# The product of q with k'v as four 64 by 64 tiles side by side, with w_in's rows permuted to match

## The chip, the cores and the metric

The kernel runs on one core of one Trainium2 chip. The metric is the device time of an execution in microseconds. The engines are named as in the profile: PE (TensorE's matmuls), PEld (its weight loads), DVE (VectorE), ACT (ScalarE), POOL (GpSimd) and SP (SyncE, which issues most of the transfers).

## The reference

Linear attention feeds a gated feed-forward layer. In float32 for the attention; the two weight matrices are float64:

```python
# q, k, v: (8 batches, 8 heads, 576 tokens, 64)
q_s = exp(q - q.max(-1));  q_s = q_s / (q_s.sum(-1) + 1e-09)     # softmax over d
k_s = exp(k - k.max(2));   k_s = k_s / (k_s.sum(2) + 1e-09)      # softmax over tokens
kv = np.einsum('bhsd,bhse->bhde', k_s, v)                        # 64 x 64 per head
x = np.einsum('bhsd,bhde->bhse', q_s, kv)
x = x.transpose(0, 2, 1, 3).reshape(4608, 512)                   # column = head * 64 + e
h = x @ w_in                                                     # w_in: 512 x 2048
g = h * erf(softplus(h))
out = g @ w_out                                                  # w_out: 2048 x 512
```

## The kernel before

**Two computations run interleaved.** The feed-forward layer goes over 48 items. An item n is a pair of batches, a block of 384 tokens (three blocks make the pair's 1152) and a quarter of the 2048 hidden columns. It has mm1 (x times its part of w_in, into the banks pX, pY, pZ), the gate in three steps (T: softplus, G: erf, both on ACT; U: the multiplication by h on DVE) and mm2 (into the banks o). The first six items use float32 matmuls (`mm1_32` at L996, mm2 at L1074); the rest split each operand into two fp16 halves and use three passes (L957, L1083). Attention for the batches b = 0 to 7 runs between: `kv_mm` (L548, 64-column tiles), `kv_norm` (L567 to L577), `kv_max`, `kv_split` (L590), the transposes of q, `x_mm` (L654) and `x_split`, in which ACT takes x out of PSUM (L449) and the fp16 halves are made.

**q times k'v.** Two heads share a block of 128 rows: x's column block c holds heads 2c and 2c + 1. `kvbd` is block diagonal: a 128 by 128 tile per c with one head's 64 by 64 k'v in the upper left, the other's in the lower right, and zeros, which POOL fills (L113, and once more at L596). `x_mm` makes one column block: q transposed (128 rows of d for two heads, 512 tokens) against that tile. For b = 0 and 1 it is one float32 matmul (L657), which the trace shows as two records; from b = 2 it is three fp16 matmuls (L660). 64 more tokens of each of two batches, the tails, are done once per pair in `tails()`, into one bank `xt`. The banks for the transposes, for x and for xt come from a pool of two (`bank`).

**The weights** come as 16 pieces of 1 MB: of w_in 256 rows by 512 columns, of w_out 256 rows. `wload` loads them, the first eight on SP's queue, the rest on POOL's, and `wdecode` on DVE turns each piece's pairs of 32-bit words into float32 (three operations, L215, L218, L221, each for 1 MB). Piece j.a is half a of the j-th job; the jobs alternate: in 0, in 1, out 0, in 2, out 1, in 3, out 2, out 3. In the prediction D2.0 or "piece 2.0" is the first half of job 2, w_out's first.

**What sets the order.** Up to item 5 the program is written out by hand in the string ORDER: a token is one step (D: decode, m: a quarter of mm1, M: a third of mm2, x: `x_mm` of batch 0, y: the rest of its split, Q: sums of squares of weights, A: the next piece of attention). After it a loop runs item by item, and `pace` takes as many pieces of attention as the numbers in SHARES say. The tile scheduler then sets the order of each engine's queue, so one step written elsewhere can move others. Every engine goes through its queue in order.

Of the kernel before, what the change touches and what calls it, by code (L numbers as in the profile page):

```python
# [8 lines left out]
F16 = mybir.dt.float16  # L9
F32 = mybir.dt.float32  # L10
# [21 lines left out]

ORDER = """
    kmax qm0 kT kB qe0 qm1 ks2 ks0 ks1 ke2 ke0 ke1 qn0 t0 t1 qe1 qn1 w6 kv0 kn0 kv1 kn1
    D0.0.0 D0.1.0 t2 t3 x0 x1 x2 x3 kvs lkv y0 y1 y2 y3
    m0.0 m0.1 D0.0.1 D0.1.1 D1.0 D1.1 m0.2 m0.3 T0 G0 Q0
    D2.0 A m1.0 D2.1 m1.1 U0 m1.2 m1.3 T1 G1 Q1 A A D3.0 M0.0 D3.1 M0.1 M0.2 Q2 U1 A A
    m2.0 D4.0 m2.1 D4.1 m2.2 m2.3 T2 G2 Q3 A A D5.0 M1.0 D5.1 M1.1 M1.2 U2 A A Q4 D6.0
# [18 lines left out]
def attn_moe_kernel(  # L57
# [9 lines left out]
    nc = tc.nc  # L67
# [95 lines left out]
    def wload():  # L163


        i = nxt[0]
        while i < NPC * NJ and slots:
            w = slots.pop(0)
            if i >= NPC * (NJ - 1 if w is None else NJ if w < 2 else w - 2):
                continue  # L170
            if w == -1:
                w, other = None, "x7"
            else:
                other = None
            which, g = wjobs[i // NPC]
            a = i % NPC
            if which == "in":
                src = w_in[a * 2 * P:(a + 1) * 2 * P, 2 * g * 512:2 * (g + 1) * 512]
            else:
                src = w_out[(4 * g + 2 * a) * P:(4 * g + 2 * a + 2) * P, :]  # L180
            if other:

                raws[i] = xp.tile([P, 2, 1024], I32, tag=other, name=f"raw_{i}")
            elif w is None:
                raws[i] = rw.bitcast(I32).rearrange("p (a n) -> p a n", a=2)
            else:
# [258 lines left out]
    def bank(name):  # L445
        return psa.tile([P, 512], F32, tag="bk", name=name)

    def x_put(src, x, s):
        nc.scalar.activation(x, src, AF.Copy, scale=2.0**-QS if s is None else s)  # L449
# [35 lines left out]
    def load_q(b, hf):  # L485
        bat[b].setdefault("q", {})[hf] = load_half(q, "q", b, hf)
# [67 lines left out]


    E32, QDMA = 2, 3
    kv32 = [t.rearrange("p h c e -> p (h c e)").bitcast(F32) for t in kvbd]
    kv32 = [t.rearrange("p (c e) -> p c e", c=NC4) for t in kv32]

    def kv_norm(b, hf, bk):  # L560
        if b >= E32:
            if hf == 0:
                bat[b]["kvf"] = asc[:, 0, :NC4 * D].rearrange("p (c e) -> p c e", c=NC4)
            kvf = bat[b]["kvf"]
# [5 lines left out]
        if b >= E32:  # L570
            nc.vector.tensor_tensor(
                kvf[:, cs, :], bkv[:, :, :D], rd.to_broadcast([P, 2, D]), op=ALU.mult
            )
            return
        for a in range(2):
            ps = slice(a * D, (a + 1) * D)
            nc.vector.tensor_tensor(  # L577
                kv32[b][ps, cs, ps], bkv[ps, :, :D], rd[ps].to_broadcast([D, 2, D]),
                op=ALU.mult,
            )  # L580

    def kv_max(b):
        mx = at.tile([P, 1], F32, tag="mx", bufs=1, name=f"mx_{b}")
        nc.vector.tensor_reduce(
            mx, (kv32[b] if b < E32 else bat[b]["kvf"]).rearrange("p c e -> p (c e)"), axis=AX.X,
            op=ALU.max, apply_absolute_value=True,
        )
        return mx

    def kv_split(b, mx):  # L590

        d = bat[b]
        s, u = scale_of_max(mx, f"x{b}")
        d["sx"], d["ux"] = s, u
        if 2 <= b < 4:
            nc.gpsimd.memset(kvbd[b % 2], 0.0)  # L596
        for a in range(2 if b >= E32 else 0):
            kvf = d["kvf"]
            ps = slice(a * D, (a + 1) * D)
            hi, lo = (kvbd[b % 2][ps, i, :, ps] for i in range(2))  # L600
            nc.vector.tensor_scalar_mul(hi, kvf[ps], s[ps])
            nc.vector.scalar_tensor_tensor(
                lo, kvf[ps], s[ps], hi, op0=ALU.mult, op1=ALU.subtract
            )
# [45 lines left out]
    def q_T(b, c, bk):  # L650
        q_cols(b, c, bk)
        return q_evac(b, c % 2, bk)

    def x_mm(b, c, out_, qT):  # L654

        if b < E32:
            nc.tensor.matmul(out_, kv32[b][:, c, :], qT[:, 0], start=True, stop=True)  # L657
            return
        for i, (wl, ql) in enumerate(((0, 0), (0, 1), (1, 0))):
            nc.tensor.matmul(  # L660
                out_, kvbd[b % 2][:, wl, c, :], qT[:, ql], start=(i == 0), stop=(i == 2)
            )

    def x_split(b, c, bk, part=None):
        for blk, off, o, w in xcols(b, 0 if b % 2 == 0 else SM + 2 * TAIL, SM)[part or slice(9)]:
            x_put(
                bk[:, o:o + w], xblock(blk)[:, c, off:off + w],
                1.0 if blk == 0 else bat[b]["sx"] if b < E32 else None,
            )

    def attention(b):
# [50 lines left out]
        def tails():  # L722
            if b < QDMA:
                bk = bank(f"qTt_{p}")
                for c in range(NC4):
                    nc.tensor.transpose(
                        bk[:, c * P:(c + 1) * P], hd(even["qt"])[:, c * P:(c + 1) * P], ident
                    )
                even["qtT"] = q_evac(b, 0, bk)
            yield SHARES[9]  # L730
            qT = even["qtT"]
            bk = bank(f"xt_{p}")
            x = xblock(p * NBK + 1)
            bk3 = bk.rearrange("p (c s) -> p c s", c=NC4)
            for a in range(2):
                for c in range(NC4):
                    cs = slice(c * P + a * TAIL, c * P + (a + 1) * TAIL)
                    x_mm(2 * p + a, c, bk[:, cs], qT[:, :, cs])
            for a in range(2 if b < E32 else 1):
                w = TAIL if b < E32 else P  # L740
                o = SM - T + a * TAIL
                x_put(
                    bk3[:, :, a * TAIL:a * TAIL + w], x[:, :, o:o + w],
                    bat[a]["sx"] if b < E32 else None,
                )
# [36 lines left out]
    def start():  # L782
# [51 lines left out]
        def xc(c):
            name = f"x_0_{c}"
            bk = pso.tile([P, 512], F32, tag=f"o{c}", name=name) if c < 3 else bank(name)
            x_mm(0, c, bk, r[f"t{c}"])
            x_split(0, c, bk, slice(1))
            put(f"x{c}", bk)

        def put(key, val):
            r[key] = val
# [392 lines left out]
```

## Time and profile before

| | |
|---|---|
| median of three runs | 847.01 us (846.93 to 848.13) |
| the profiled execution's own time | 847.39 us |
| its span in the profile | 845.4 us |
| granted clock of TensorE | 1.0 |
| DMA, whole span | 61.53 MB, mean 73 GB/s |
| w_in's first pieces on SP's queue, issue to landing | 10.6 us (median of 4) |

The span runs from the first to the last instruction of the profiled execution; its time holds about 2 us around that. Rows of groups read: line, engine, operation, result and operands, shapes, count; busy time in us and mean ns of one; idle time of the engine before them and what ended it. Timeline rows read: start in us, us, engine, line, operation. Neighbouring matmuls overlap, so one's own cost is the distance of the starts.

### The profile page before, as it was taken

To read this page: it belongs to the slowest core of one execution; us is meant where nothing else is said; L and a number is where in the kernel's file an instruction comes from. 1 tells how busy PE (TensorE), PEld (TensorE's weight loads), DVE (VectorE), ACT (ScalarE), POOL (GpSimd) and SP (SyncE) were. 2 spreads that over 40 slices of the span, in tenths; PEclk is the share of its full clock that TensorE was granted. 3 is DMA by queue.
4 is the path that set the end of the run, shared out by engine and by line. 5 is a ranking of instruction groups with operands and counts; after the bars stand their busy time and mean duration, and the time that the engine had idled before them with its cause. 6 is when DMAs were issued, how large, how long until landed. Compare 5 with 4: busy or idle time off the path is not lost.

```text
span 845.4 us, 15123 instructions
## 1 busy us (share of the span) xinstructions
PE 817.5 (97%) x6336; PEld 554.3 (66%) x6336; DVE 631.9 (75%) x900; ACT 506.6 (60%) x638; POOL 18.1 (2%) x37
## 2 busy tenths in 40 slices
PE   3999999999999999999999999999999999999996
PEld 2655555666766766766776776766776776767662
DVE  6899689998998869867877769867876657553543
ACT  2597659876674567465665467465665475544532
POOL 2101100000000000000000000000000000000000
PEclk9999999999999999999999999999999999999999
DMA  9975920023226303411171203411131100100100
GB/s 267 403 189 168 210 52 38 1 58 75 63 51 127 88 19 76 106 38 27 46 151 30 76 19 76 106 39 26 40 74 13 40 1 1 39 1 2 38 1 38
DMA packets 141347, 61.53 MB, mean 73 GB/s; under 512 B 130528, under 2 KB 132576, under 8 KB 141280
## 3 DMA queue, kind: packets, MB, share of 16 engines
q1 hardware_dynamic: 139104, 52.18, 24.9%
q0 software_dynamic: 2176, 8.39, 2.9%
q8 instruction: 50, 0.82, 0.4%
q14 instruction: 17, 0.14, 0.1%
HBM read 45.09 MB, written 9.44 MB: 64 GB/s over the span
## 4 chain that ended last, share of the span: by engine, by line
PE 66%; DVE 16%; ACT 10%; DMA 3%; issue 3%; SPq 1%; POOL 0%; ACTq 0%; DVEq 0%; POOLq 0%
PE o L1083 28%; PE pX L957 15%; PE pZ L957 8%; PE o L1074 4%; ACT G L350 3%; PE pY L957 3%; ACT L350 3%; DVE G L1037 2%; PE kv L548 2%; DVE H L1055 2%; DMA q<-in_q_dram 1%; PE x L660 1%; SPq L415 1%; ACT wt L301 1%; DVE wt L302 1%
## 5 line engine op out<-in xcount | busy, mean ns | idle before, releaser
L1083 PE MATMUL o<-wt,H 128*128 128x512 f16 x1512 | 347.4, 379 | 1.8 <-DVE H L1051 1.3
L957 PEld LDWEIGHTS <-wt 128*128 128x128 f16 x3528 | 294.0, 98 | 29.3 <-issue 5.6
L1083 PEld LDWEIGHTS <-H 128*128 128x128 f16 x1512 | 145.9, 98 | 150.8 <-DVE H L1051 1.8
L957 PE MATMUL pX<-x,wt 128*128 128x192 f16 x2016 | 193.9, 246 | 1.8 <-ACT H L976 0.7
L350 ACT ACT_TABLE_LOAD x105 | 134.7, 1283 | 3.2 <-DVE H L982 1.2
L1037 DVE SCALAR_TENSOR_TENSOR G<-G,small,H 128x1536 f32<-128x1536 f32 x44 | 79.9, 1817 | 46.2 <-ACT G L350 45.9
L984 ACT COPY H<-pX 128x384 f32<-128x384 f32 x42 | 20.0, 477 | 136.8 <-PE pX L957 131.4
L957 PE MATMUL pZ<-x,wt 128*128 128x192 f16 x1008 | 98.2, 246 | 0.0
L350 ACT ACTIVATE G<-H,U 128x768 f32<-128x768 f32 (+1 forms) x56 | 69.3, 1255 | 22.1 <-DVE H L982 21.5
L1055 DVE TENSOR_TENSOR H<-G,H 128x1536 f16<-128x1536 f32 x42 | 73.8, 1756 | 1.0
L350 ACT ACTIVATE G<-G 128x1536 f32<-128x1536 f32 x48 | 71.3, 1486 | 0.5
L449 ACT ACTIVATE x<-x 128x384 f32<-128x384 f32 (+1 forms) x52 | 17.7, 388 | 59.4 <-PE x L660 56.9
L957 PE MATMUL pY<-x,wt 128*128 128x192 f16 x504 | 48.4, 246 | 0.0
L982 DVE TENSOR_TENSOR H<-pZ,H 128x384 f32<-128x384 f32 x42 | 23.2, 553 | 28.9 <-PE pZ L957 28.9
L301 ACT ACTIVATE x<-x 128x768 f16<-128x768 f32 (+1 forms) x44 | 32.9, 762 | 16.4 <-DVE x L394 16.3
L969 DVE COPY H<-pY 128x384 f32<-128x384 f32 x42 | 23.3, 554 | 25.8 <-PE pY L957 25.8
L1051 DVE CAST H<-G 128x1536 f16<-128x1536 f32 x42 | 40.2, 957 | 0.8
L302 DVE SCALAR_TENSOR_TENSOR x<-x,x 128x768 f16<-128x768 f32 (+1 forms) x44 | 37.4, 853 | 3.2 <-ACT x L301 3.2
L1099 DVE TENSOR_SCALAR ob<-o,V 128x512 f32<-128x512 f32 x29 | 21.7, 749 | 21.9 <-PE o L1083 21.8
L996 PE MATMUL pX<-x,wt 128*128 128x384 f32 x96 | 33.9, 488 | 0.0
L971 DVE TENSOR_TENSOR H<-pX,H 128x384 f32<-128x384 f32 x42 | 23.3, 555 | 13.3 <-PE pX L957 12.5
L460 DVE TENSOR_REDUCE q_m<-q 128x16 f32<-128x1024 f32 x14 | 17.1, 1219 | 17.9 <-DMA q<-in_q_dram 17.9
(182 smaller groups left out, 851.1 us busy)
## 6 DMA issues: line engine op xcount, KB each, us to landing
out_dram<-ob SPq DMA_DIRECT2D x32, 256.0 KB, 2.3
vbuf<-in_v_dram SPq DMA_DIRECT2D x60, 128.0 KB, 3.2
q<-in_q_dram SPq DMA_DIRECT2D x56, 128.0 KB, 3.3
k<-in_k_dram SPq DMA_DIRECT2D x56, 128.0 KB, 3.4
wt<-in_moe_w_out_dram POOLq DMA_DIRECT2D x5, 1024.0 KB, 8.7
wt<-in_moe_w_in_dram SPq DMA_DIRECT2D x4, 1024.0 KB, 10.6
wt<-in_moe_w_out_dram SPq DMA_DIRECT2D x2, 1024.0 KB, 15.6
H_raw<-in_k_dram SPq DMA_DIRECT2D x2, 512.0 KB, 5.0
```

The source lines that it names most:

```text
L301: nc.scalar.activation(hi, src, AF.Copy, scale=s)
L302: nc.vector.scalar_tensor_tensor(lo, src, s, hi, op0=ALU.mult, op1=ALU.subtract)
L350: i = nc.scalar.activation(out_, in_, func, **kw)
L957: nc.tensor.matmul(o, w[wl][:, c, a * P:(a + 1) * P], x[:, xl, xi, c, :], start=(new and a == 0 and c == 0 and i == 0), stop=(c == 1 and i ...
L969: nc.vector.tensor_copy(C[0, 0], bank2("Y"))
L971: add(C[0, 0], bank2("X"), C[0, 0], op=ALU.add)
L996: nc.tensor.matmul(ph[:, :T], w[:, c, a * P:(a + 1) * P], x[:, c, :], start=(c == 0), stop=(c == NC4 - 1),)
L1037: nc.vector.scalar_tensor_tensor(flat(s["G"]), flat(s["G"]), GA32 if n < N32 else GA[:, g:g + 1], flat(s["H"]), op0=ALU.mult, op1=ALU.mult,)
L1051: nc.vector.tensor_copy(flat(s["gh"]), flat(s["G"]))
L1055: nc.vector.tensor_tensor(flat(s["gl"]), flat(s["G"]), flat(s["gh"]), op=ALU.subtract)
L1074: nc.tensor.matmul(o, s["G"][:, a, ts_], w[:, a, :], start=(first_ and a == 0), stop=(last_ and a == FG - 1),)
L1083: nc.tensor.matmul(o, s[gt][:, a, ts_], w[wl][:, a, :], start=(first_ and a == 0 and i == 0), stop=(last_ and a == FG - 1 and i == 2),)
```

## The change

`kvbd` becomes `kvh`, which is dense: the 128 partitions hold two heads' 64 rows each, with 64 columns and no zeros. `x_mm` now makes two column blocks, a half hf of x, at once: each pass has four matmuls of 64 rows by 64 columns, one per head. Head 2c + a takes row half a of PE, column half c, and writes bank a. So bank a's partitions hold head a of the first block and head a of the second: the order of x's columns within a half is changed, and w_in's rows are loaded in that order, each piece by two transfers of 64 partitions where one of 128 did it. `kv_norm` is one operation on 128 partitions, `kv_split` two. `x_split` of both blocks follows the product. The loop over the column blocks becomes one over the halves: two transposed q's, then the product. The tails use two banks. In ORDER the tokens x1 and x3 go, and x0 and x2 wait for two transposes each.

```diff
-    D0.0.0 D0.1.0 t2 t3 x0 x1 x2 x3 kvs lkv y0 y1 y2 y3
+    D0.0.0 D0.1.0 t2 t3 x0 x2 kvs lkv y0 y1 y2 y3
...
-    kvbd = []
-    for i in range(2):
-        t = cp.tile([P, 2, NC4, P], F16, name=f"kvbd{i}")
-        nc.gpsimd.memset(t, 0.0)
-        kvbd.append(t)
+    kvh = [cp.tile([P, 2, NC4, D], F16, name=f"kvh{i}") for i in range(2)]
...
-            eng.dma_start(raws[i], src.rearrange("(a p) n -> p a n", p=P))
+            if which == "in":
+                for c in range(2):
+                    eng.dma_start(
+                        raws[i][c * D:(c + 1) * D],
+                        src[c * P:(c + 1) * P].rearrange("(a p) n -> p a n", p=D),
+                    )
+            else:
+                eng.dma_start(raws[i], src.rearrange("(a p) n -> p a n", p=P))
...
-        for a in range(2):
-            ps = slice(a * D, (a + 1) * D)
-            nc.vector.tensor_tensor(
-                kv32[b][ps, cs, ps], bkv[ps, :, :D], rd[ps].to_broadcast([D, 2, D]),
-                op=ALU.mult,
-            )
+        nc.vector.tensor_tensor(
+            kvf[:, cs, :], bkv[:, :, :D], rd.to_broadcast([P, 2, D]), op=ALU.mult
+        )
...
-        if 2 <= b < 4:
-            nc.gpsimd.memset(kvbd[b % 2], 0.0)
-        for a in range(2 if b >= E32 else 0):
-            kvf = d["kvf"]
-            ps = slice(a * D, (a + 1) * D)
-            hi, lo = (kvbd[b % 2][ps, i, :, ps] for i in range(2))
-            nc.vector.tensor_scalar_mul(hi, kvf[ps], s[ps])
+        if b >= E32:
+            hi, lo = (kvh[b % 2][:, i] for i in range(2))
+            nc.vector.tensor_scalar_mul(hi, d["kvf"], s)
...
-    def x_mm(b, c, out_, qT):
-
-        if b < E32:
-            nc.tensor.matmul(out_, kv32[b][:, c, :], qT[:, 0], start=True, stop=True)
-            return
-        for i, (wl, ql) in enumerate(((0, 0), (0, 1), (1, 0))):
-            nc.tensor.matmul(
-                out_, kvbd[b % 2][:, wl, c, :], qT[:, ql], start=(i == 0), stop=(i == 2)
-            )
+    def x_mm(b, hf, outs, qTs):
+
+        passes = ((0, 0),) if b < E32 else ((0, 0), (0, 1), (1, 0))
+        for i, (wl, ql) in enumerate(passes):
+            for c in range(2):
+                for a in range(2):
+                    ps = slice(a * D, (a + 1) * D)
+                    w = kv32[b][ps, 2 * hf + c] if b < E32 else kvh[b % 2][ps, wl, 2 * hf + c]
+                    nc.tensor.matmul(
+                        outs[a][c * D:(c + 1) * D], w, qTs[c][ps, ql],
+                        start=(i == 0), stop=(i == len(passes) - 1),
+                    )
...
-        for c in range(NC4):
-            hf, c2 = divmod(c, 2)
-            if c == 2 and j == 1 and b >= QDMA:
+        for hf in range(2):
+            if hf == 1 and j == 1 and b >= QDMA:
                 yield from tails()
...
-            bk = bank(f"x_{b}_{c}")
-            x_mm(b, c, bk, qT)
...
+            bks = [bank(f"x_{b}_{hf}_{a}") for a in range(2)]
+            x_mm(b, hf, bks, qTs)
...
-            x_split(b, c, bk)
-            if c == NC4 - 1:
+            for a in range(2):
+                x_split(b, 2 * hf + a, bks[a])
+            if hf == 1:
                 d["xdone"] = True
-            yield SHARES[12]
+            yield 2 * SHARES[12]
```

The scheduler's order moves with it, in places that the diff doesn't touch. The first is DVE's queue while item 0 is at its gate; wt are buffers of weights, G and H item 0's gate and mm1. Before, the multiplication of G by H stands behind pieces 2.0, 2.1 and most of what follows:

```order
L215 TENSOR_SCALAR wt_95<-wt_96 128x1024
L218 SCALAR_TENSOR_TENSOR wt_95<-wt_96,wt_95 128x1024
L215 TENSOR_SCALAR wt_95<-wt_97 128x1024
L221 SCALAR_TENSOR_TENSOR wt_95<-wt_96,wt_95 128x1024
L218 SCALAR_TENSOR_TENSOR wt_95<-wt_97,wt_95 128x1024
L215 TENSOR_SCALAR wt_96<-wt_98 128x1024
L221 SCALAR_TENSOR_TENSOR wt_95<-wt_97,wt_95 128x1024
L218 SCALAR_TENSOR_TENSOR wt_96<-wt_98,wt_96 128x1024
L215 TENSOR_SCALAR wt_97<-rw 128x1024
L1034 TENSOR_TENSOR G_377<-G_377,H_337 128x1536
```

In the changed kernel the same place on DVE, from piece 2.0 on (here wt_93):

```order
L220 TENSOR_SCALAR wt_93<-wt_94 128x1024
L1044 TENSOR_TENSOR G_384<-G_384,H_343 128x1536
L223 SCALAR_TENSOR_TENSOR wt_93<-wt_94,wt_93 128x1024
L220 TENSOR_SCALAR wt_93<-wt_95 128x1024
L226 SCALAR_TENSOR_TENSOR wt_93<-wt_94,wt_93 128x1024
L223 SCALAR_TENSOR_TENSOR wt_93<-wt_95,wt_93 128x1024
L226 SCALAR_TENSOR_TENSOR wt_93<-wt_95,wt_93 128x1024
```

The multiplication has moved ahead of five of the six operations on pieces 2.0 and 2.1.

The second place is DVE's queue at the scale of batch 1 (x_s is the scale by which ACT multiplies as it takes x out; rw a weight buffer whose source wt waits for a transfer). Before:

```order
L142 RECIPROCAL x_s<-x_e 128x1
L144 TENSOR_SCALAR x_u<-x_e 128x1
L221 SCALAR_TENSOR_TENSOR sg_653<-wt_92,sg_653 128x1024
L143 TENSOR_SCALAR x_s<-x_s 128x1
L215 TENSOR_SCALAR rw<-wt_91 128x1024
```

And in the changed kernel, where the scale's last operation stands behind the first on rw:

```order
L139 RECIPROCAL x_s<-x_e 128x1
L141 TENSOR_SCALAR x_u<-x_e 128x1
L220 TENSOR_SCALAR rw<-wt_89 128x1024
L140 TENSOR_SCALAR x_s<-x_s 128x1
L223 SCALAR_TENSOR_TENSOR rw<-wt_89,rw 128x1024
```

The operation on rw and the scale's last one have changed places.

More of the change, by code (lines that the diff above doesn't have):

```diff
@@ L556, in attn_moe_kernel @@
     E32, QDMA = 2, 3
-    kv32 = [t.rearrange("p h c e -> p (h c e)").bitcast(F32) for t in kvbd]
+    kv32 = [t.rearrange("p h c e -> p (h c e)").bitcast(F32) for t in kvh]
     kv32 = [t.rearrange("p (c e) -> p c e", c=NC4) for t in kv32]
     def kv_norm(b, hf, bk):
[L561 to L564, printed above, removed]
+        if b < E32:
+            kvf = kv32[b]
+        else:
+            kvf = asc[:, 0, :NC4 * D].rearrange("p (c e) -> p c e", c=NC4)
+        bat[b]["kvf"] = kvf
         bkv = bk[:, :2 * W].rearrange("p (c w) -> p c w", c=2)
@@ L569, in kv_norm @@
         cs = slice(2 * hf, 2 * hf + 2)
-        if b >= E32:
-            nc.vector.tensor_tensor(
-                kvf[:, cs, :], bkv[:, :, :D], rd.to_broadcast([P, 2, D]), op=ALU.mult
-            )
-            return
-        for a in range(2):
-            ps = slice(a * D, (a + 1) * D)
-            nc.vector.tensor_tensor(
-                kv32[b][ps, cs, ps], bkv[ps, :, :D], rd[ps].to_broadcast([D, 2, D]),
-                op=ALU.mult,
-            )
+        nc.vector.tensor_tensor(
+            kvf[:, cs, :], bkv[:, :, :D], rd.to_broadcast([P, 2, D]), op=ALU.mult
+        )
     def kv_max(b):
@@ L584, in kv_max @@
         nc.vector.tensor_reduce(
-            mx, (kv32[b] if b < E32 else bat[b]["kvf"]).rearrange("p c e -> p (c e)"), axis=AX.X,
+            mx, bat[b]["kvf"].rearrange("p c e -> p (c e)"), axis=AX.X,
             op=ALU.max, apply_absolute_value=True,
@@ L594, in kv_split @@
         d["sx"], d["ux"] = s, u
-        if 2 <= b < 4:
-            nc.gpsimd.memset(kvbd[b % 2], 0.0)
-        for a in range(2 if b >= E32 else 0):
-            kvf = d["kvf"]
-            ps = slice(a * D, (a + 1) * D)
-            hi, lo = (kvbd[b % 2][ps, i, :, ps] for i in range(2))
-            nc.vector.tensor_scalar_mul(hi, kvf[ps], s[ps])
+        if b >= E32:
+            hi, lo = (kvh[b % 2][:, i] for i in range(2))
+            nc.vector.tensor_scalar_mul(hi, d["kvf"], s)
             nc.vector.scalar_tensor_tensor(
-                lo, kvf[ps], s[ps], hi, op0=ALU.mult, op1=ALU.subtract
+                lo, d["kvf"], s, hi, op0=ALU.mult, op1=ALU.subtract
             )
@@ L652, in q_T @@
         return q_evac(b, c % 2, bk)
-    def x_mm(b, c, out_, qT):
-        if b < E32:
-            nc.tensor.matmul(out_, kv32[b][:, c, :], qT[:, 0], start=True, stop=True)
-            return
-        for i, (wl, ql) in enumerate(((0, 0), (0, 1), (1, 0))):
-            nc.tensor.matmul(
-                out_, kvbd[b % 2][:, wl, c, :], qT[:, ql], start=(i == 0), stop=(i == 2)
-            )
+    def x_mm(b, hf, outs, qTs):
[9 more added lines that the diff above has]
+                    )
     def x_split(b, c, bk, part=None):
@@ L731, in tails @@
             qT = even["qtT"]
-            bk = bank(f"xt_{p}")
+            bks = [bank(f"xt_{p}_{a}") for a in range(2)]
             x = xblock(p * NBK + 1)
-            bk3 = bk.rearrange("p (c s) -> p c s", c=NC4)
-            for a in range(2):
-                for c in range(NC4):
[L737 to L745, printed above, removed]
+            for j_ in range(2):
+                for hf in range(2):
+                    oc = slice(hf * P + j_ * TAIL, hf * P + (j_ + 1) * TAIL)
+                    qs_ = [
+                        qT[:, :, (2 * hf + c) * P + j_ * TAIL:(2 * hf + c) * P + (j_ + 1) * TAIL]
+                        for c in range(2)
+                    ]
+                    x_mm(2 * p + j_, hf, [bk[:, oc] for bk in bks], qs_)
+            w = TAIL if b < E32 else P
+            for a, bk in enumerate(bks):
+                bk3 = bk[:, :2 * P].rearrange("p (f s) -> p f s", f=2)
+                for j_ in range(P // w):
+                    o = SM - T + j_ * TAIL
+                    x_put(
+                        bk3[:, :, j_ * TAIL:j_ * TAIL + w], x[:, a::2, o:o + w],
+                        bat[j_]["sx"] if b < E32 else None,
+                    )
             if b + 1 < B:
@@ L751, in attention @@
             yield from tails()
-        for c in range(NC4):
-            hf, c2 = divmod(c, 2)
-            if c == 2 and j == 1 and b >= QDMA:
+        for hf in range(2):
+            if hf == 1 and j == 1 and b >= QDMA:
                 yield from tails()
-            qT = q_T(b, c, bank(f"qT_{b}_{c}")) if b < QDMA else d["qT"][c]
-            if b < QDMA and c2 == 1 and b + 1 < B:
-                load_q(b + 1, hf)
-            yield SHARES[11]
-            bk = bank(f"x_{b}_{c}")
-            x_mm(b, c, bk, qT)
-            if b >= QDMA and c2 == 1 and b + 1 < B:
-                load_q(b + 1, hf)
-            x_split(b, c, bk)
-            if c == NC4 - 1:
+            qTs = []
+            for c in (2 * hf, 2 * hf + 1):
+                qTs.append(q_T(b, c, bank(f"qT_{b}_{c}")) if b < QDMA else d["qT"][c])
+                if b < QDMA and c % 2 == 1 and b + 1 < B:
+                    load_q(b + 1, hf)
+                yield SHARES[11]
+            bks = [bank(f"x_{b}_{hf}_{a}") for a in range(2)]
+            x_mm(b, hf, bks, qTs)
+            if b >= QDMA and b + 1 < B:
+                load_q(b + 1, hf)
+            for a in range(2):
+                x_split(b, 2 * hf + a, bks[a])
+            if hf == 1:
                 d["xdone"] = True
-            yield SHARES[12]
+            yield 2 * SHARES[12]
     def attention_rest():
@@ L832, in qn, with xc @@
             q_norm(rows(d["q"][hf]), 16, f"q_0_{hf}", 0)
[L834 to L839, printed above, removed]
+        def xc(hf):
+            bks = []
+            for c in (2 * hf, 2 * hf + 1):
+                name = f"x_0_{c}"
+                bks.append(
+                    pso.tile([P, 512], F32, tag=f"o{c}", name=name) if c < 3 else bank(name)
+                )
+            x_mm(0, hf, bks, [r[f"t{2 * hf + c}"] for c in range(2)])
+            for a in range(2):
+                x_split(0, 2 * hf + a, bks[a], slice(1))
+                put(f"x{2 * hf + a}", bks[a])
         def put(key, val):
@@ L880, in start @@
             steps[f"t{i}"] = (f"qn{i // 2}" + (f" t{i - 1}" if i else ""), lambda i=i: tc_(i))
-            steps[f"x{i}"] = (f"t{i} kn1", lambda i=i: xc(i))
-            steps[f"y{i}"] = (f"x{i} kvs", lambda i=i: x_split(0, i, r[f"x{i}"], slice(1, 9)))
+            if i % 2 == 0:
+                steps[f"x{i}"] = (f"t{i} t{i + 1} kn1", lambda i=i: xc(i // 2))
+            steps[f"y{i}"] = (f"x{i - i % 2} kvs", lambda i=i: x_split(0, i, r[f"x{i}"], slice(1, 9)))
         return steps
```

## The prediction

> **What bounds the kernel now.** I read the page's busy shares first, then the chain that ended last, then the busy time by stretch.
>
> ```profile
> PE 817.5 (97%) x6336; PEld 554.3 (66%) x6336; DVE 631.9 (75%) x900; ACT 506.6 (60%) x638; POOL 18.1 (2%) x37
> ...
> PE 66%; DVE 16%; ACT 10%; DMA 3%; issue 3%; SPq 1%; POOL 0%; ACTq 0%; DVEq 0%; POOLq 0%
> ...
> 27.00:60.00 33.00, 33.00 (x95) 17.23 (x94) 32.57 (x47) 28.37 (x56) 2.30 (x3) 1.00 0.96 302
> 60.00:90.00 30.00, 29.38 (x156) 15.75 (x155) 29.73 (x45) 22.15 (x36) 3.55 (x5) 1.00 0.52 154
> ...
> 220.00:400.00 180.00, 176.99 (x1551) 124.94 (x1549) 145.14 (x215) 110.41 (x134) 1.27 (x4) 1.00 0.30 68
> 400.00:600.00 200.00, 199.79 (x1743) 142.12 (x1742) 153.18 (x220) 118.60 (x139) 1.27 (x4) 1.00 0.26 60
> 600.00:832.00 232.00, 230.58 (x1920) 161.56 (x1918) 136.34 (x172) 124.55 (x138) 0.00 (x0) 1.00 0.09 23
> ```
>
> The window rows give the stretch and its length, then the busy time of PE, of PE's weight loads, DVE, ACT and POOL, the granted clock, the DMA share and the rate. From 220 on PE idles 4.6 of 612 us (180 − 176.99, 200 − 199.79, 232 − 230.58) at full clock: what is taken off PE there comes off the end. From 27 to 60 PE is full too, but DVE is busy 32.57 of 33.00: what DVE waits for there cannot be caught up, so it can make a hole in PE. These two stages I cost apart.
>
> **The x products after b = 1 (gain).** What shrinks stands in the groups of instructions by shape, and in the timeline of PE:
>
> ```profile
> L660 PE MATMUL x<-q,kvbd 128*128 128x512 f16 x60 | 16.4, 379 | 0.9 <-DVE kvbd L601 0.6 <-DVE kvbd L602 0.3
> L660 PE MATMUL x<-asc,kvbd 128*128 128x512 f16 x12 | 3.4, 379 | 1.6 <-DVE asc L639 1.6
> ...
> 477.95 0.81 PE L660 MATMUL x<-q,kvbd 128*128 128x512 f16 x3
> 478.59 0.58 PE L957 MATMUL pX<-x,wt 128*128 128x192 f16 x5
> ...
> 622.01 2.75 PE L1083 MATMUL o<-wt,H 128*128 128x512 f16 x12
> 624.70 0.69 PE L548 MATMUL kv<-vbuf,k 128*64 128x65 f32 x16
> 625.33 0.64 PE L548 MATMUL kv<-vbuf,k 128*64 128x65 f32 x16
> 625.80 0.29 PE L548 MATMUL kv<-vtail,kt 128*64 128x65 f32 x4
> 626.01 0.42 PE L957 MATMUL pZ<-x,wt 128*128 128x192 f16 x3
> ```
>
> The 72 matmuls are six batches times four column blocks times three passes. Three take 478.59 − 477.95 = 0.64 us, 0.216 each. Two blocks are now done together: before 6 × 0.216 = 1.30; after, 12 matmuls of 64 × 64, four per pass. If the four run side by side a pass is 0.216 and the three 0.65. The trace has no 64-row tiles; it has 64-column ones. Of the kv products 16 records take 0.64, of which the last alone about 0.22, so they begin 28 ns apart. A 65-column f32 record would by the 512-column f32 rows below (0.86 per call in two records, 0.84 ns a column) take 55, so two columns of tiles do run side by side. The bounds of a pass are thus 0.216 (all four) and 0.432 (only columns pair). I take 0.216: rows and columns are the same kind of split, and the two banks and disjoint rows leave nothing shared.
>
> That the packing holds for rows too is what the Trainium skill says, "TensorE: Matmul & The Clock Gate", Part 3, "The mechanism": tiles in different rows and columns start about 4 ns apart and run together; no run here shows rows, and by it the pass is 0.216 plus some 12 ns.
>
> Going in and out of tiled mode has a price. From 622.01 twelve matmuls of 0.216 end at 624.60, and the kv products begin at 624.70: 0.09. On the way out, 625.80 to 626.01, four records of 28 ns need 0.11 and the next begins 0.10 later than that. Together 0.19 per group, and as much per tail. So a group gains 1.30 − 0.65 − 0.02 − 0.19 = 0.44; twelve groups (b from 2 to 7, two each) **−5.3 us**.
>
> The tails, 24 matmuls of 64 columns in one bank, become 48 small ones in two banks. They are short before and after:
>
> ```profile
> L660 PE MATMUL xt<-qt,kvbd 128*128 128x64 f16 x72 | 2.6, 193 | 0.0
> L449 ACT ACTIVATE x<-x 128x384 f32<-128x384 f32 x28 | 13.6, 486 | 32.4 <-PE x L660 30.0 <-PE x L657 2.4
> L449 ACT ACTIVATE x<-x 128x128 f32<-128x128 f32 x24 | 6.6, 274 | 26.9 <-PE x L660 26.9
> ```
>
> Three tails cost +0.1 in all (the mode price against some halved passes). But a tail now needs both banks of the pool of two, and at b = 5 and 7 the group of x products stands right before it: it waits until ACT has taken both x banks out, 2 × (0.486 + 0.274) = 1.52 us, under which only eight matmuls of mm1 (8 × 0.083 = 0.66) stand. The second bank's wait is thus 0.86 a tail; **+1.7** for two. Cover that would hide it is nothing, since PE goes in order; if the tail's first bank alone bound, it would be 0.1.
>
> **Waits that go.** kvbd's split was four DVE operations on 64 partitions and is two on 128; the normalisation two, now one:
>
> ```profile
> L571 DVE TENSOR_TENSOR asc<-kv,rd 128x128 f32<-128x128 f32 x12 | 3.3, 273 | 0.1
> L577 DVE TENSOR_TENSOR kvbd<-kv,rd 64x128 f32<-64x128 f32 x8 | 2.3, 284 | 0.1
> L601 DVE TENSOR_SCALAR kvbd<-asc,x_s 64x256 f16<-64x256 f32 x12 | 4.2, 348 | 0.2
> L602 DVE SCALAR_TENSOR_TENSOR kvbd<-asc,x_s,kvbd 64x256 f16<-64x256 f32 x12 | 5.8, 479 | 0.3
> ```
>
> An operation's time goes with its row, not its partitions (128 partitions 273, 64 partitions 284), so the split falls from 1.65 to 0.83 us per batch, and the 0.9 us that PE waited for it (first row of L660) go. At b = 2, PE waited 1.6 us for asc; now two transposes stand ahead of the product, but both banks must come free: I take half, −0.8. Together **−1.7**; bounds 0 and −2.5. The zero fills go from POOL, 2% busy, at nothing.
>
> **The start (loss).** For b = 0 and 1 the products are f32, and PE does less:
>
> ```profile
> L657 PE MATMUL x<-asc,kvbd 128*128 128x512 f32 x10 | 5.1, 592 | 0.0
> L657 PE MATMUL x<-qTs,kvbd 128*128 128x512 f32 x6 | 2.9, 592 | 0.0
> L657 PE MATMUL xt<-asc,kvbd 128*128 128x64 f32 x16 | 2.0, 278 | 0.0
> ```
>
> Eight calls of 0.86 (two records each) become four groups: −3.4, and the tail about −0.9. That alone would be −4.3. But the order of DVE moves. The gate's last multiply of item 0 (G by H, 128x1536) stood behind the decoding of the next weights; now it stands behind the first operation of piece 2.0. What it waits for:
>
> ```profile
> 41.73 0.46 ACT L1000 COPY H<-pX 128x384 f32<-128x384 f32 x1
> 42.21 1.28 ACT L350 ACT_TABLE_LOAD   x1
> 43.51 1.49 ACT L350 ACTIVATE G<-H 128x1536 f32<-128x1536 f32 x1
> ...
> 45.62 1.28 ACT L350 ACT_TABLE_LOAD   x1
> 46.92 1.49 ACT L350 ACTIVATE G<-G 128x1536 f32<-128x1536 f32 x1
> ...
> 40.28 0.69 DVE L215 TENSOR_SCALAR wt<-wt 128x1024 int32<-128x1024 int32 x1
> ...
> 42.76 1.22 DVE L221 SCALAR_TENSOR_TENSOR wt<-wt,wt 128x1024 int32<-128x1024 int32 x1
> ...
> 48.51 1.76 DVE L1034 TENSOR_TENSOR G<-G,H 128x1536 f32<-128x1536 f32 x1
> ...
> 51.51 10.46 PE L1074 MATMUL o<-wt,G 128*128 128x512 f32 x24
> 61.81 2.74 PE L996 MATMUL pX<-x,wt 128*128 128x384 f32 x8
> ```
>
> ACT's chain from the copy of H to the erf's end is 41.73 to 48.41. DVE came to its multiply at 48.51 with four more pieces begun; piece 2.0's first operation was its row at 40.28. After, by a walk through the new order with these durations, that operation ends at 42 to 43, and DVE stands until ACT ends, about 6 us, with the rest of 2.0 and all of 2.1 queued behind it. Their five operations (1.22 for the long ones, 0.69 for the short, a little overlapped) end some 5.2 us after a multiply that ends at about 51: 56.3. mm2 of item 0 (M0), 24 matmuls in 10.3 us, reads both pieces in halves; its second half cannot begin before 56.3, and 56.3 plus 5.1, with what its last groups still wait for, is mm1 of item 2 at some 64.9 in place of 61.81: +3.1. Of it the f32 savings at b = 1 and the transposes of k that now fill M0's gaps give back 1.2 by item 3. The second place is b = 1's scale: its last operation (x_s) now stands behind the first operation of a weight piece that waits for its load.
>
> ```profile
> 95.79 0.15 DVE L143 TENSOR_SCALAR x_s<-x_s 128x1 f32<-128x1 f32 x1
> 101.69 0.69 DVE L215 TENSOR_SCALAR rw<-wt 128x1024 int32<-128x1024 int32 x1 [5.75 <-DMA wt<-in_moe_w_out_dram]
> 102.42 0.77 PE L657 MATMUL xt<-asc,kvbd 128*128 128x64 f32 x5
> ```
>
> x_s came at 95.79 and would come after 102.4; b = 1's tail, at 102.42 on PE, cannot leave its banks without it. With two banks per group that is 1.6 more. So the start is 3.1 − 1.2 + 1.6 = **+3.5**. Bounds: −2 (half of the f32 savings, all waits covered) and +9 (6 us of DVE standing, 3 for the coupled banks). I take the value of the walk, between them.
>
> **w_in's loads** are two transfers of 64 partitions each, for one of 128. The rate now (per slice of 15 to 30 us):
>
> ```profile
> GB/s 214 202 212 282 382 382 382 448 415 382 448 404 404 448 415 415 393 415 448 382 415 426 404 393 426 404 404 426 393 404 426 393 448 393 371 404 393 426 415 393
> ```
>
> A MB takes 2.6 us. No row shows a half load of this size: bounds nothing and, at half the rate, 2.6 us more per w_in piece, 10 us by the fourth. I take nothing; decoding of the first pieces begins some us behind their landing, and the rest is a rival.
>
> **Sum**, against the profiled execution's own 847.4 (span 845.4): −5.3 + 0.1 + 1.7 − 1.7 + 3.5 = −1.7, so 845.7. That execution is 0.4 above the median of its runs: **845.3**.
>
> **Rivals.**
> - *The start costs nothing*: PE's saving of 4.3 covers DVE's standing. Then 845.3 − 3.5 = 841.8. For it speaks that PE had no hole there before; against it, DVE's 32.57 of 33.00.
> - *Slower by DVE's order*: the multiply of item 0 holds the decoding for the whole 6 us and M0 waits all of it, +7 in place of +3.5: 848.8. Against the gains of 5.2 it decides once the start costs more than that. For it speaks that DVE from 60 to 90 is busy 29.73 of 30, so nothing is caught up until 90; against it that PE's own work shrinks meanwhile.
> - *The change doesn't do what it says*: rows don't run side by side, only columns. A pass is 0.432, a group 1.30 + 0.19, twelve cost +2.3 in place of −5.3, and the f32 groups save nothing (+1.7 in the start): 845.3 + 7.6 + 1.7 = 854.6. All four in sequence the kv rows exclude.
> - *Half-rate loads*: piece 1.1, which landed at about 27, lands 10 us later, and DVE was at it at about 36; item 1 begins later, and later pieces too: +3, 848.3. For it nothing in this trace; most of what comes late stands behind the multiply anyway.
>
> On that last the Trainium skill is plain, "SBUF — State Buffer", "Can I just issue two DMAs to hit both halves?": two transfers, to partitions from 0 and from 64, gained 6% over one and go in sequence, each at its own ports' rate. By it the 1 MB takes nearly twice as long; no row here shows it, and the sum by it would be 848.3.
>
> **Chances.** Forecast 0.48; start free 0.17; DVE's order 0.20; rows in sequence 0.08; loads 0.07. The range takes in the start's bounds on both sides, −2 and +9: 839.8 to 850.8, rounded 840 to 851, and leaves out the rows in sequence and the ends. A measurement of this kernel tells about 0.2% (1.7 us) from no change. Half of the forecast's case and most of the free start lie below 845.3; the rest of the forecast's and part of the loads' within; the slower cases are DVE's order and rows in sequence: faster 0.43, same 0.29, slower 0.28.
>
> **What would show it.** Right: groups of x products of 0.65 us from 130 us on, twelve in all; a pause of 0.8 before the tails of b = 5 and 7; a DVE gap of some 6 us ahead of the multiply of item 0, and mm1 of item 2 at about 65. Wrong: groups of 1.3 us, w_in pieces landing 5 us apart, no DVE gap there, or a gap that PE does not feel.

## The result: slower by 0.7%, and the profile after

| | before | changed |
|---|---|---|
| median | 846.94 us (7 runs, 844.77 to 848.13) | 853.30 us (7 runs, 850.06 to 854.41) |
| ratio | | 1.0074, 95% interval 1.0055 to 1.0093 |
| profiled execution, its span | 847.39, 845.4 us | 851.74, 849.7 us |
| granted clock, profiled execution | 1.0 | 0.992 |

The forecast was 845.3, in a range up to 851.0. The time is 8.0 us above the one and outside the other.

The same views of the changed kernel, the page's busy shares and chain first:

```profile
PE 815.2 (96%) x6512; PEld 547.3 (64%) x6512; DVE 625.3 (74%) x884; ACT 504.1 (59%) x642; POOL 14.8 (2%) x35
...
PE 64%; DVE 13%; ACT 9%; DMA 7%; SPq 4%; issue 2%; ACTq 0%; DVEq 0%
```

And its busy time by stretch (columns as before):

```profile
27.00:60.00 33.00, 30.10 (x90) 15.22 (x83) 25.55 (x36) 24.36 (x47) 4.25 (x6) 1.00 1.05 283
60.00:90.00 30.00, 27.31 (x74) 13.69 (x73) 26.92 (x31) 20.99 (x40) 1.44 (x2) 0.94 0.90 196
```

PE is busy 2.3 us less over the run, yet the span is 4.3 us longer. In the chain DMA grew from 3% to 7% and SP's queue from 1% to 4%. Between 27 and 60 us DVE fell from 32.57 busy to 25.55: it waits, and PE with it.

What it waits for shows in the rate of the transfers from 17 to 32 us, the stretch of w_in's first pieces; first the changed kernel, then the one before:

```profile
DMA packets 899, 3.29 MB, mean 219 GB/s; under 512 B 99, under 2 KB 99, under 8 KB 898
```

```profile
DMA packets 1599, 6.17 MB, mean 412 GB/s; under 512 B 95, under 2 KB 95, under 8 KB 1598
```

A transfer to 64 partitions moves 219 GB/s where one to 128 moved 412: a MB of w_in costs 4.8 us and not 2.5. This is what the Trainium skill says in "SBUF — State Buffer", "Can I just issue two DMAs to hit both halves?": the halves go in sequence. The trace agrees: the two halves of a piece together move 219 GB/s.

Behind those pieces on SP's queue stand batch 1's q and k. Their issues, in the changed kernel and then in the one before (start of the first, length of all eight):

```profile
34.62 27.57 SPq L420 DMA_DIRECT2D q<-in_q_dram  x8
...
68.41 8.90 SPq L420 DMA_DIRECT2D k<-in_k_dram  x8
```

```profile
23.83 24.32 SPq L415 DMA_DIRECT2D q<-in_q_dram  x8
...
49.54 5.66 SPq L415 DMA_DIRECT2D k<-in_k_dram  x8
```

In the changed kernel DVE waits for the fourth piece of w_in (0.40), for a piece of w_out (1.18), for the gate on ACT (5.06), for the tail of q (1.70) and for k (0.42), and then PE waits for DVE's work on k (timelines of DVE and of PE, the wait in brackets):

```profile
37.13 0.70 DVE L220 TENSOR_SCALAR wt<-wt 128x1024 int32<-128x1024 int32 x1 [0.40 <-DMA wt<-in_moe_w_in_dram]
...
41.53 0.70 DVE L220 TENSOR_SCALAR wt<-wt 128x1024 int32<-128x1024 int32 x1 [1.18 <-DMA wt<-in_moe_w_out_dram]
47.28 1.76 DVE L1044 TENSOR_TENSOR G<-G,H 128x1536 f32<-128x1536 f32 x1 [5.06 <-ACT G L355]
...
75.56 0.69 DVE L465 TENSOR_REDUCE qt_m<-qt 128x8 f32<-128x512 f32 x1 [1.70 <-DMA qt<-in_q_dram]
77.79 0.69 DVE L508 TENSOR_TENSOR asc<-k 128x512 f32<-128x512 f32 x1 [0.42 <-DMA k<-in_k_dram]
```

```profile
63.05 1.45 PE L1006 MATMUL pX<-x,wt 128*128 128x384 f32 x4
...
85.32 1.12 PE L519 MATMUL kT<-ident,asc 128*128 128x128 f32 x4 [2.52 <-DVE asc L512]
86.23 3.03 PE L1084 MATMUL o<-wt,G 128*128 128x512 f32 x4
89.09 0.60 PE L532 MATMUL kB<-ident,km 128*128 128x128 f32 x4
...
154.72 1.15 PE L967 MATMUL pY<-x,wt 128*128 128x192 f16 x12
```

mm1 of item 2 begins at 63.05, 1.2 us later than before (61.81). Then PE stands 2.5 us ahead of the transposes of k. Item 6, the first row of L967, begins at 154.72. Before:

```profile
149.21 1.15 PE L957 MATMUL pY<-x,wt 128*128 128x192 f16 x12
```

So 5.5 us are lost by then. The rest of the program should have won 5.2 back and won 0.5: the last row of matmuls starts 5.05 us later than before (839.17 against 834.12).

### The profile page after: what moved, and what is told of

It is laid out like the page before. It is cut to its first block, busy times and chain, and to the rows that moved or that the text cites. A ratio compares the mean times of both kernels' runs of the same rounds, so it can differ in the third digit from the quotient of the medians.

```text
span 849.7 us, 15479 instructions
## 1 busy us (share of the span) xinstructions
PE 815.2 (96%) x6512; PEld 547.3 (64%) x6512; DVE 625.3 (74%) x884; ACT 504.1 (59%) x642; POOL 14.8 (2%) x35
## 4 chain that ended last, share of the span: by engine, by line
PE 64%; DVE 13%; ACT 9%; DMA 7%; SPq 4%; issue 2%; ACTq 0%; DVEq 0%
PE o L1093 28%; PE pX L967 15%; PE pZ L967 7%; DMA wt<-in_moe_w_in_dram 4%; PE pY L967 3%; ACT G L355 3%; ACT L355 3%; PE o L1084 2%; SPq L420 2%; DVE G L1047 2%; DVE H L1065 2%; PE kv L553 2%; PE pX L1006 2%; DVE x L307 1%; PE x L657 1%
## 5 line engine op out<-in xcount | busy, mean ns | idle before, releaser
L967 PEld LDWEIGHTS <-wt 128*128 128x128 f16 x3528 | 294.5, 98 | 37.2 <-issue 15.3
L967 PE MATMUL pX<-x,wt 128*128 128x192 f16 x2016 | 195.1, 247 | 6.3 <-DVE H L989 4.1
L967 PE MATMUL pZ<-x,wt 128*128 128x192 f16 x1008 | 98.5, 246 | 0.0
L967 PE MATMUL pY<-x,wt 128*128 128x192 f16 x504 | 49.3, 249 | 0.0
L1006 PEld LDWEIGHTS pX<-x,wt 128*128 128x128 f32 x96 | 17.4, 190 | 16.6 <-ACT H L1010 3.1
```

The costliest lines, as they stand in the source:

```text
L967: nc.tensor.matmul(o, w[wl][:, c, a * P:(a + 1) * P], x[:, xl, xi, c, :], start=(new and a == 0 and c == 0 and i == 0), stop=(c == 1 and i ...
L1006: nc.tensor.matmul(ph[:, :T], w[:, c, a * P:(a + 1) * P], x[:, c, :], start=(c == 0), stop=(c == NC4 - 1),)
```

## The experiments

Each run's ratio is against runs of the kernel before on the same chip.

### The loads alone, and as many loads on all partitions

The theory: the two-part load of w_in is the whole loss. First the kernel before with that load only:

```diff
-            eng.dma_start(raws[i], src.rearrange("(a p) n -> p a n", p=P))
+            sp = src.rearrange("(a p) n -> p a n", p=P)
+            for c in range(2):
+                eng.dma_start(raws[i][c * D:(c + 1) * D], sp[c * D:(c + 1) * D])
```

> The kernel before with only w_in's pieces loaded as two transfers of 64 partitions each (natural row order, the same numbers in the end). Theory L (the half-partition loads make the start late: 2.4 us per half MB, the batch-1 loads behind them on SP's queue, and the order that the scheduler makes of it): 851 to 853 us, a MB of w_in takes 4.8 us, the gate's multiply of item 0 stands in DVE's queue after a wait of about 5 us, a PE hole of 2 to 3 us near 83 to 85 us ahead of batch 1's transposes of k, item 6 begins 4 to 6 us later than in the kernel before. Rival O (the loop by halves and the coupled banks make the start late): 846 to 848 us, item 6 within 1 us of before.

Measured: 856.5 us, ratio 1.0127 (1.0103 to 1.0152): 10.3 us lost by the loads alone (by the medians), more than expected. PE from item 2 to the start of item 6:

```profile
65.19 1.13 PE L1001 MATMUL pX<-x,wt 128*128 128x384 f32 x3
...
90.95 1.11 PE L519 MATMUL kT<-ident,asc 128*128 128x128 f32 x4 [5.91 <-DVE asc L512]
...
161.34 1.15 PE L962 MATMUL pY<-x,wt 128*128 128x192 f16 x12
```

Item 6 is 12.1 us late (161.34 against 149.21), and the hole ahead of k's transposes is 5.9 us long. The profiled execution took 861.9 us, the longest of the six, so these rows show more than the median loses. The gate's multiply of item 0 moved ahead of pieces 2.0 and 2.1 here too, with nothing else changed, and DVE stood there:

```profile
49.42 1.76 DVE L1039 TENSOR_TENSOR G<-G,H 128x1536 f32<-128x1536 f32 x1 [6.70 <-ACT G L355]
```

The order that the prediction had put down to the change as a whole is thus the scheduler's answer to the slow loads.

The control has as many transfers per piece, each over 128 partitions:

```diff
-            eng.dma_start(raws[i], src.rearrange("(a p) n -> p a n", p=P))
+            for a_ in range(2):
+                eng.dma_start(raws[i][:, a_], src[a_ * P:(a_ + 1) * P])
```

> The kernel before with each w_in piece as two transfers over all 128 partitions (512 KB each, one per block of 128 rows): as many transfers as in the changed kernel, on twice the partitions. Theory P (64 partitions take half the rate): 846 to 848 us, 512 KB in 1.3 us. Rival N (it is the number of transfers, by their issue on SP's queue): 851 us or more, 512 KB in 2.4 us.

Measured: 846.7 us, ratio 1.0004 (0.9996 to 1.0013). The gate's multiply of item 0 keeps its place behind pieces 2.0 and 2.1 (48.23 us; in the kernel before 48.51). So it is not the number of transfers that costs, but the 64 partitions.

### The changed kernel without the half loads

x's columns can come out in natural order if each row half of the tiles holds two neighbouring heads. Then w_in is loaded as before:

```diff
-                    h = 2 * c + a
+                    h = 2 * a + c
...
+            sl = 2 * (h % 2) + h // 2 if tag == "q" else h
-            eng.dma_start(t[:, h, :, :D] if tag == "v" else t[:, :, h, :], s4[:, h])
+            eng.dma_start(t[:, h, :, :D] if tag == "v" else t[:, :, sl, :], s4[:, h])
```

(q's first raw load becomes two transfers, and the tails' q is put in the same order as it is cast or transposed.)

> The changed kernel with w_in loaded as before the change (one transfer of 128 partitions per piece, natural row order); x's columns come out in natural order because each row half of the tiles now holds two neighbouring heads (kv's products and q's head slots are paired 0 with 2 and 1 with 3). Four tiles side by side, two banks and the loop by halves stay. Theory L (the half-partition loads are what made the change slow): 841 to 846 us, item 6 no later than 1 us after that of the kernel before, no PE hole of over 1.5 us between 30 and 130 us. Rival O (banks and loop): 850 us or more, the lag at item 6 over 4 us.

Measured: 843.0 us, ratio 0.9963 (0.9949 to 0.9977). Against the changed kernel that is 1.11%, 9.4 us: within the noise of the two ratios, the half loads cost from this side what they cost alone. Item 6 begins 1.6 us earlier than in the kernel before, and DVE is full again:

```profile
27.00:60.00 33.00, 32.41 (x104) 16.69 (x97) 32.76 (x45) 28.68 (x55) 2.29 (x3) 1.00 0.97 305
...
147.61 1.15 PE L978 MATMUL pY<-x,wt 128*128 128x192 f16 x12
```

### The loop by halves alone, and where q's load stands

Of the 5.2 us that the later stages should have won, the changed kernel shows little. PE stood 2.2 us at 312:

```profile
309.33 1.15 PE L967 MATMUL pZ<-x,wt 128*128 128x192 f16 x12
312.71 1.15 PE L967 MATMUL pX<-x,wt 128*128 128x192 f16 x12 [2.23 <-DVE H L989]
313.70 2.02 PE L967 MATMUL pY<-x,wt 128*128 128x192 f16 x12
```

DVE had waited 3.1 us for a load of q. On SP's queue that load stands behind two output stores; in the kernel before its first transfer is ahead of the second. The changed kernel, then before:

```profile
294.37 2.78 SPq L1112 DMA_DIRECT2D out_dram<-ob  x2
297.26 2.62 SPq L420 DMA_DIRECT2D q<-in_q_dram  x4
```

```profile
290.77 0.34 SPq L1102 DMA_DIRECT2D out_dram<-ob  x1
291.33 0.58 SPq L415 DMA_DIRECT2D q<-in_q_dram  x1
293.22 0.33 SPq L1102 DMA_DIRECT2D out_dram<-ob  x1
293.60 2.69 SPq L415 DMA_DIRECT2D q<-in_q_dram  x3
```

The kernel before with the loop by halves only (block-diagonal products kept):

```diff
-            bk = bank(f"x_{b}_{c}")
-            x_mm(b, c, bk, qT)
+            bks = [bank(f"x_{b}_{hf}_{a}") for a in range(2)]
+            for a in range(2):
+                x_mm(b, 2 * hf + a, bks[a], qTs[a])
```

> The kernel before with only attention's loop changed for batches 1 to 7: both transposed q's of a half first, then both 128-row products against the block-diagonal tile, then both evictions, the next q's load behind both. Theory Q (that loop puts the load of the next q behind an output store on SP's queue, so that DVE waits for it and PE stands 2 us or more near 310 us): 849 to 851 us, with that hole. Rival T (the hole belongs to the tiles' shorter time, not to the loop): 846 to 848 us, no stall of PE over 1 us near 310 us.

Measured: 848.8 us, ratio 1.0028 (1.0018 to 1.0039). The time came near theory Q's, the hole did not: PE's longest stall near there is 1.1 us, at 301. So the loop costs 1.5 to 3.3 us, but how is left open by this run; its profiled execution, 846.8 us, was also the fastest of the seven.

The stores moved to POOL's queue, once with natural w_in loads and once in the changed kernel itself:

```diff
-                nc.sync.dma_start(dst, src)
+                (nc.gpsimd if p < B // 2 - 1 else nc.sync).dma_start(dst, src)
```

> The same with the output stores of the first three batch pairs issued on POOL's queue, so that no load of q stands behind a store on SP's. Theory Q (the 2.4 us hole near 312 us of the changed kernel is a q load behind a store): 1 to 3 us less than the run with paired heads on SP alone, and no PE stall of over 1.5 us from 280 to 330 us. Rival (the hole is that run's own order on DVE): within 1 us of it.

> The changed kernel, half-partition loads and all, with the output stores of the first three batch pairs issued on POOL's queue. Theory Q (the load of the next q behind an output store makes the PE hole near 312 us): 2 to 4 us below the changed kernel (849 to 851), no PE hole of over 1.5 us between 280 and 330 us. Rival (the hole is DVE's own order): within 1 us of 853.

Measured: 841.4 us, ratio 0.9946 (0.9934 to 0.9959), 1.6 us under the run without it; and 852.0, ratio 1.0062 (1.0050 to 1.0074), 1.3 under the changed kernel, which is not clear of the noise (its ratio is 1.0055 to 1.0093) and less than the 2 to 4 expected. The place in question with paired heads, stores on SP and then on POOL:

```profile
301.92 1.15 PE L978 MATMUL pZ<-x,wt 128*128 128x192 f16 x12
304.84 1.15 PE L978 MATMUL pX<-x,wt 128*128 128x192 f16 x12 [1.77 <-DVE H L1000]
```

```profile
303.80 1.15 PE L978 MATMUL pZ<-x,wt 128*128 128x192 f16 x12
305.05 1.15 PE L978 MATMUL pX<-x,wt 128*128 128x192 f16 x12
```

The stall of 1.77 is gone (0.10 between the two rows), and in the changed kernel with the stores on POOL no stall over 0.8 us is left from 280 to 330. Theory Q holds for the hole. In that last run the profile shows the gain too, but only from item 6 on: to the last row of matmuls it takes 681.0 us (158.24 to 839.27) against 684.5 in the changed kernel (154.72 to 839.17). What it wins there it had lost at the start, where item 6 began 3.5 us later and the hole ahead of k's transposes was 3.7 us long, against 2.5; why the start was slower is open. 841.4 us is the best time of this study, 4.5 below the kernel before.

### Which half loads cost

The same half load for the later pieces only (`i >= 4`), then for the first four only (`i < 4`), in the kernel before.

> The kernel before with half-partition loads for the later w_in pieces only (jobs in 2 and in 3: two pieces on SP's queue, two on POOL's). DVE's order at item 0's gate stays that of the kernel before. Theory S (each MB at half rate moves everything behind it on SP's queue 2.2 us back; batch 1's k had about 6 us of slack before DVE needs it at 61 us): k lands 4 to 5 us later and the slack takes it, 846 to 848 us. Rival A (each half-rate MB costs its 2.2 us at once): 850 to 855 us.

> The kernel before with half-partition loads for the first four w_in pieces only (jobs in 0 and in 1). DVE's order at item 0's gate becomes that of the changed kernel (the multiply ahead of pieces 2.0 and 2.1), and k of batch 1 lands 9 to 10 us later, 3 to 4 us past its slack. Theory S (slack, then a PE hole ahead of batch 1's transposes of k): 849 to 852 us, that hole 2 to 3 us long, mm1 of item 2 at most 2 us late. Rival G (DVE's order at the gate is most of the 10 us): 854 to 857 us, mm1 of item 2 over 4 us late.

Measured: 851.8 (ratio 1.0073, 1.0055 to 1.0090) and 855.3 (1.0107, 1.0092 to 1.0122). Theory S missed both, and both times lie in the rivals' ranges (A: 850 to 855, G: 854 to 857), though mm1 of item 2 came 3.85 us late in the second (65.66 against 61.81) and G wanted over 4. The slack of k is not what is used up first. In the first of them DVE kept its old order, and the order itself became the trap:

```profile
46.46 0.69 DVE L220 TENSOR_SCALAR wt<-rw 128x1024 int32<-128x1024 int32 x1
50.81 0.69 DVE L220 TENSOR_SCALAR wt<-wt 128x1024 int32<-128x1024 int32 x1 [3.65 <-DMA wt<-in_moe_w_out_dram]
51.42 1.22 DVE L223 SCALAR_TENSOR_TENSOR wt<-rw,wt 128x1024 int32<-128x1024 int32 x1
52.56 1.75 DVE L1039 TENSOR_TENSOR G<-G,H 128x1536 f32<-128x1536 f32 x1
```

The multiply now stands behind the first operation of a piece that lands late, DVE waits 3.65 us, and PE's mm2 of item 0 began 2.9 us later than before. In the second the multiply went ahead, and DVE waited 6.70 us for ACT as in the first run. The two runs lose 5.3 and 8.7 us, together more than the 10.3 of both edits at once; DVE's queue is held up at the gate in either order, which may be why they don't add up. How much of the loss is the rate alone and how much the order that the scheduler makes of it, these runs don't separate.

### Two attempts at whole loads

The permuted rows as two transfers of 128 partitions each, straight from w_in, the two 64-row groups as the outermost dimension of the source:

```diff
+                sp = src.rearrange("(c a p) n -> c p a n", c=2, p=D)
+                for a_ in range(2):
+                    eng.dma_start(raws[i][:, a_], sp[:, :, a_])
```

> The changed kernel with each w_in piece loaded as two transfers over all 128 partitions (one per block of rows) in the same permuted order; all else as in the changed kernel. Theory L: the start's lag of 5.5 us goes, 845.5 to 848 us against 853.3, item 6 within 1.5 us of the kernel before, no PE hole near 85 us. Rival O: 851 to 854 us, the lag at item 6 stays at 4 us or more.

Measured: 963.2 us, ratio 1.138 (1.136 to 1.139). The stretch from 17 to 57 us:

```profile
17.00:57.00 40.00, 13.23 (x103) 7.99 (x103) 9.60 (x21) 5.99 (x10) 1.54 (x3) 0.63 0.13 52
```

The DMA share is 0.13 of 16 engines, about two of them, at 52 GB/s. The transfers did not get their full rate, so the run tells nothing of either theory. It agrees with the Trainium skill, "DMA: Bandwidth & Descriptors", "Rules for kernel authors": a source whose outermost dimension has c entries is spread over c engines at most, and here c is 2.

Then the half loads of the kernel before, the upper half on POOL's queue:

```diff
-                    eng.dma_start(raws[i][c * D:(c + 1) * D], sp[c * D:(c + 1) * D])
+                    (eng, nc.gpsimd)[c].dma_start(raws[i][c * D:(c + 1) * D], sp[c * D:(c + 1) * D])
```

> The kernel before with half-partition w_in loads as in the first run, but the upper half of each of the first pieces issued on POOL's queue, the lower on SP's, so that both halves of a piece can be in flight together. Theory F (the loss comes from one queue's order: while one half's 64 partitions fill, the rest of the bandwidth stands idle): the two halves of a piece land within 1.5 us of each other, a piece costs 2.6 to 3.2 us, 846 to 850 us. Rival H (two queues share the engines and their halves still go in sequence, as the Trainium skill, SBUF - State Buffer, Can I just issue two DMAs to hit both halves?, says): a piece still costs 4.4 us or more, 852 us or more.

Measured: 874.8 us, ratio 1.0335 (1.0319 to 1.0352). POOL's transfers began at 3.9 us and ran beside the first loads of q and v, which came late; DVE waited 7.45 us for one of them. From 12 to 27 us both queues were at work:

```profile
12.00:27.00 15.00, 1.56 (x8) 0.75 (x6) 7.45 (x10) 3.80 (x4) 1.90 (x1) 1.00 1.09 222
```

222 GB/s is no more than one queue's half loads. But the two halves of one piece were never in flight together, so neither theory was put to the test.

## Why the prediction was wrong

**The step that failed is the price of w_in's loads.** It was written as "bounds nothing and, at half the rate, 2.6 us more per w_in piece, 10 us by the fourth. I take nothing", and as a rival of chance 0.07 and +3. The rate was that of the dear bound (219 against 412 GB/s). A piece took 4.8 us, and pieces landing 5 us apart were one of the signs named for being wrong. The cost was 9.4 us in the changed kernel and 10.3 alone. The bound was seen and its consequence mis-sized. The piece was checked against its own first reader, and there the argument held: the reader of the fourth piece waited 0.40 us. So that the loss comes near the bound's 10 us is chance, as far as the runs show. What was not checked is the queue behind the pieces (batch 1's q and k on SP, first issued 10.8 and 18.9 us later) and the scheduler: its order on DVE moved with the shape of the loads alone. That it goes by an estimate of when a load lands is inferred.

**The start's +3.5 had the wrong cause.** "The order of DVE moves" was right, and DVE stood (5.06 us against "about 6"). Yet with full loads and the rest of the change in place the multiply stood behind pieces 2.0 and 2.1 again, DVE did not wait for ACT ahead of it, and item 6 began 1.6 us early: of the start's own cost nothing was left. That run's 843.0 us is nearest to the rival of the free start, 841.8. Item 2 began 1.2 us late, not 3.1; the larger loss came later, ahead of k's transposes, which no term named. And x_s behind a weight piece, priced at 1.6, cost nothing that the trace shows: that piece had landed. The f32 products gave less than the 3.4 us taken: batch 0's two groups take 1.88 us (25.73 to 27.61) for four calls of 0.86, but batch 1's take 1.50 each (114.12 to 115.62) and not 0.86; its tail gained 1.2 (0.62 for 1.83) where 0.9 was taken.

**The x products after b = 1 were sized right, each by itself.** Four tiles do run side by side, rows too. A group in the paired-heads run, then the tail that follows:

```profile
456.78 0.81 PE L1104 MATMUL o<-wt,H 128*128 128x512 f16 x3
457.52 0.84 PE L665 MATMUL x<-q,kvh 64*64 64x512 f16 x12
458.30 0.83 PE L978 MATMUL pX<-x,wt 128*128 128x192 f16 x8
459.12 1.12 PE L665 MATMUL xt<-qt,kvh 64*64 64x64 f16 x48
460.17 0.50 PE L978 MATMUL pX<-x,wt 128*128 128x192 f16 x4
```

The three matmuls ahead end at 456.78 + 0.65 = 457.43, the group at 458.30: 0.87 with the changes of mode, against 1.30. That is 0.43 gained, and 0.44 was forecast (the 0.02 in that sum stands on no row). All twelve groups of the changed kernel have this length. By the medians, loop, tiles and tails together are −0.37%, the loop alone +0.28%, so the rest −0.65%, some 5.5 us, give or take 1.5; the f32 groups and the start are in it as well, so that it comes near the −5.3 of the sum says little.

Less of it reached the end. From item 6 to the last row of matmuls the kernel before takes 684.9 us, the changed one 684.5, paired heads 682.2 and with the stores on POOL 681.2: 0.5, 2.8 and 3.7 of the 5.2 forecast for the later stages. One term that fell short is **the waits that go** (−1.7): PE's 1.6 us for asc and 0.9 for kvbd did go, but beside batch 2's groups it now waits 0.91 for DVE to take mm1 out of its bank (209.88) and 0.69 for ACT to take x out (217.83).

**The tail was half as dear.** It takes 1.05 us where it took 0.70, and starts 0.16 after the eight matmuls: +0.5, between the two cases that were priced, 0.1 and 0.86.

**What the sum did not have** is the loop: it loses 1.5 to 3.3 us by itself, and how is open. With the tiles there is also the q load behind an output store; with the stores on another queue 1.6 us come back in the run with paired heads. The prediction followed the moved steps on PE and DVE, and not SP's queue.

## What to carry to other kernels

A change of layout in a compute step can be paid where the data is laid out, as here: look first at what it does to the loads, in partitions per transfer, and then at everything queued behind them. The layout can sometimes be had for nothing further up; here pairing other heads gave the same tiles and left the load alone, and 853.3 became 843.0 us. Where a scheduler orders the queues, a slower load can also move instructions that never touch it.

## What the runs showed of the hardware that was not expected

After some holes in PE the granted clock fell to half. The changed kernel, around its hole of 2.5 us at 83 to 85 and that of 2.2 us at 312 (TensorE's clock is the third number from the end):

```profile
84.00:86.00 2.00, 0.68 (x3) 0.68 (x4) 1.94 (x3) 1.99 (x3) 0.00 (x0) 0.78 0.91 356
86.00:88.00 2.00, 2.00 (x6) 0.97 (x5) 2.00 (x3) 1.94 (x6) 0.00 (x0) 0.50 0.06 25
88.00:90.00 2.00, 2.00 (x9) 1.19 (x8) 1.10 (x2) 1.95 (x4) 0.00 (x0) 0.87 0.00 0
...
314.00:316.00 2.00, 2.00 (x15) 1.88 (x14) 0.25 (x1) 1.97 (x3) 0.00 (x0) 0.50 0.00 0
316.00:318.00 2.00, 2.00 (x15) 1.58 (x13) 0.78 (x2) 1.98 (x2) 0.00 (x0) 0.70 0.00 0
```

In those stretches twelve matmuls of L967 took 2.02 us (313.70) and the next twelve 1.99 (315.51), not the usual 1.15; the transposes kT took 1.12 (85.32) where kB, of the same shape, took 0.60 (89.09), and four matmuls of mm2 3.03 (86.23) where eight took 3.60 before (98.85). So each hole cost another 1.5 to 1.7 us behind it. The Trainium skill tells of such a gate in "TensorE: Matmul & The Clock Gate", Part 1, with an idle window of about 3.4 us; here shorter holes were enough.

But the length of a hole alone does not decide it. Between 13 and 21 us both kernels have two holes, of 2.42 and 3.04 us in the one before and of 2.42 and 3.42 in the changed one, and only the changed one's clock falls (before, then changed):

```profile
18.00:21.00 3.00, 0.68 (x13) 0.71 (x14) 2.79 (x5) 2.00 (x2) 0.18 (x1) 1.00 1.03 416
```

```profile
18.00:21.00 3.00, 1.23 (x17) 1.14 (x18) 2.81 (x4) 1.67 (x2) 0.00 (x0) 0.50 1.02 224
```

A hole of 2.1 us, at 238 us in the run with paired heads and the stores on POOL, was not followed by a lower clock either. What decides it these runs don't show.
